# Loads moved to GpSimd's queue and stores to ACT's in a linear-attention and feed-forward kernel

## The chip, the cores and the metric

The kernel runs on one core of one Trainium2 chip. The metric is the device time of one execution in microseconds (us), as the median of several runs. Engines are PE (matmul), DVE (vector), ACT (scalar), POOL (GpSimd) and SP (sync, which here only issues transfers).

## The reference

```python
def phi(x):
    return np.where(x > 0, x, np.exp(x) - 1.0) + 1.0
q_p, k_p = phi(q), phi(k)                      # q, k, v: (8, 8, 576, 64) float32
kv  = np.einsum('bhsd,bhse->bhde', k_p, v)
z   = np.sum(k_p, axis=2)
num = np.einsum('bhsd,bhde->bhse', q_p, kv)
den = np.einsum('bhsd,bhd->bhs', q_p, z)[..., None] + 1e-06
x   = (num / den).transpose(0, 2, 1, 3).reshape(4608, 512)
h   = x @ w_in                                 # w_in: (512, 2048)
g   = 0.5 * h * (1.0 + np.tanh(np.sqrt(2 / np.pi) * (h + 0.044715 * h ** 3)))
out = g @ w_out                                # w_out: (2048, 512)
```

## The kernel before

Eight batches pass through a pipeline of first halves (x times w_in, then GELU) and second halves (g times w_out). A second half also prepares the attention of a batch two ahead. A main load is 512 of the 576 rows of one batch, 1 MB for each of q, k and v. The other 64 rows of two batches share one "remainder" tile. After GELU of half j the plan runs the functions that are registered for a slot (1 or 2 for first or second half, j, slot).

```python
def load_batch(b):                                   # all on SP
    if b % 2 == 0:
        ld["kr", b // 2] = load_rest(k, b // 2, "k_r", nc.sync)
    ld["k", b] = load_main(k, b, "k_x", nc.sync)
    ld["q", b] = load_main(q, b, "q_x", nc.sync)
    ...                                              # v and the remainders of v and q alike
def qtr():                                           # the transposed q of a batch, by DMA on SP
    phis("q")
    qts[b] = pt.tile([P, C, NP, P], BF16, name="qt")
    for c in range(C):
        nc.sync.dma_start_transpose(out=qts[b][:, c], in_=phi["q", b][:, c].rearrange(...))
def tx(c):                                           # the transposed x, by DMA on SP
    nc.sync.dma_start_transpose(out=xts[b][:, :, P * c : P * (c + 1)], in_=box["x", c]...)
def store(j, t, o_sb):                               # 512 KB of output, on GpSimd
    nc.gpsimd.dma_start(out=ov[:, t - 1 : t + 1, :], in_=o_sb)
...
at(1, 1, 15, lambda: load_batch(3))
plan_rest(0, (2, 1, 12), 2, 14)
for b in range(4, B):
    at(2, b - 3, 13 if b == 4 else 0, lambda b=b: load_batch(b))
```

Six load buffers of 1 MB are in rotation, so a load of batch b+2 can start as soon as the same load of batch b has been used. DMA transposes all go through SP's queue, in order.

## Time and profile before

| | before |
|---|---|
| time, median of three runs | 318.54 us (316.97 to 319.39) |
| PE busy | 290.1 us, 91% of a span of 318.6 us |
| DVE, ACT, POOL busy | 126.5, 153.9 and 27.8 us |
| mean granted PE clock | 0.970 |
| longest waits of PE | first GELU 7.5 us, transposed q of batch 4 6.4 us |

PE is the bound; what can be won is what it waits. The prediction shows the slices, the waits and the timelines. Two more lines: the table of DMA queues (packets, MB, share of 16 engines' time) and the table of DMA issues (count, median us from issue to landing).

```profile
q1 hardware_dynamic: 71968, 42.87, 49.1%
...
qt<-q_p SPq DMA_TRANSPOSE x24, 2.6
```

SP's queue, q1, carries nearly everything, and in the median a q transpose lands 2.6 us after its issue.

### The profile page before, as it was taken

Reading aid. Unit: us, or ns where it says so; the run is one execution under the profiler, and the core shown is the slowest. Engines: PE = TensorE matmul, PEld = TensorE weight load, DVE = VectorE, ACT = ScalarE, POOL = GpSimd, SP = SyncE. Lnnn points to the kernel's source line nnn. Section 1 sums busy time; section 2 is a strip of 40 time slices with the busy share of each in tenths; the row PEclk is TensorE's granted clock in tenths of the full one; section 3 lists DMA queues with packets and bytes.
Section 4 is the critical chain, followed back from the end, with each engine's and each line's share of the span. In section 5 each row is a group of like instructions: output and inputs, shape, how many; then the busy total and the mean of one; then the engine's idle time right before and its main releaser. Section 6 shows DMA issues by size and latency. Waiting matters only on the chain.

```text
span 318.6 us, 4203 instructions
## 1 busy us (share of the span) xinstructions
PE 290.1 (91%) x1624; PEld 147.7 (46%) x1652; DVE 126.5 (40%) x242; ACT 153.9 (48%) x214; POOL 27.8 (9%) x44
## 2 busy tenths in 40 slices
PE   8774588999999999929999999999999999999994
PEld 6552145444554544504445544544454444444443
DVE  3957255007787335912191439335523000000001
ACT  4636544678323576412844683557355036207500
POOL 6042261000000000000000000000100000000000
PEclk9998599999999999996999999999999999999998
DMA  7999999850484798993499259530623120011032
GB/s 246 343 377 260 386 328 321 270 177 0 144 171 128 191 340 118 300 260 84 109 357 262 49 153 359 134 60 6 137 74 66 43 95 0 2 66 67 0 68 68
DMA packets 75509, 52.72 MB, mean 165 GB/s; under 512 B 44128, under 2 KB 69984, under 8 KB 75488
## 3 DMA queue, kind: packets, MB, share of 16 engines
q1 hardware_dynamic: 71968, 42.87, 49.1%
q0 software_dynamic: 3360, 9.44, 9.5%
q8 instruction: 13, 0.21, 0.3%
q10 hardware_dynamic: 160, 0.13, 0.2%
q14 instruction: 8, 0.07, 0.1%
HBM read 36.70 MB, written 9.44 MB: 145 GB/s over the span
## 4 chain that ended last, share of the span: by engine, by line
PE 80%; DMA 11%; ACT 4%; DVE 2%; SPq 1%; issue 1%; DVEq 0%
PE o_ps L624 38%; PE h_ps L295 37%; DMA q_x<-in_q_dram 4%; DMA qt<-q_p 4%; PE n_ps L247 3%; DMA k_r<-in_k_dram 3%; PE kv_ps L212 2%; ACT g L587 1%; DMA out_dram<-o_sb 1%; SPq L67 1%; DVE vr L204 1%; ACT xt L548 1%; PE kv_ps L220 0%; ACT L140 0%; ACT kr_e L186 0%
## 5 line engine op out<-in xcount | busy, mean ns | idle before, releaser
L295 PE MATMUL h_ps<-xt,w_in_sb 128*128 128x512 bf16 (+1 forms) x513 | 124.1, 382 | 10.9 <-ACT g L587 8.2
L624 PE MATMUL o_ps<-w_out_sb,g 128*128 128x512 bf16 x548 | 122.5, 379 | 0.6
L587 ACT ACTIVATE g<-h_ps 128x512 bf16<-128x512 f32 x144 | 85.5, 598 | 62.7 <-PE h_ps L295 61.4
L295 PEld LDWEIGHTS <-w_in_sb 128*128 128x128 bf16 x592 | 56.7, 99 | 69.0 <-issue 16.5
L624 PEld LDWEIGHTS <-g 128*128 128x128 bf16 x560 | 54.5, 98 | 64.5
L638 ACT COPY o_sb<-o_ps 128x512 f32<-128x512 f32 x17 | 9.9, 585 | 66.4 <-issue 33.9
L636 DVE COPY o_sb<-o_ps 128x512 f32<-128x512 f32 x18 | 12.3, 685 | 63.0 <-PE o_ps L624 62.2
L565 POOL DMA_DIRECT2D out_dram<-o_sb x16 | 9.3, 584 | 229.9 <-DVE o_sb L636 120.2
L259 DVE TENSOR_TENSOR x<-n_ps,r 128x512 bf16<-128x512 f32 x36 | 24.9, 691 | 7.9 <-DMA xt<-x 6.5
L164 DVE TENSOR_SCALAR k_e<-k_e 128x2048 bf16<-128x2048 bf16 (+1 forms) x9 | 6.5, 717 | 41.0 <-ACT k_e L159 36.4
L257 DVE RECIPROCAL r<-n_ps 128x8 f32<-128x8 f32 x36 | 7.4, 206 | 36.4 <-PE n_ps L247 36.4
L168 DVE SCALAR_TENSOR_TENSOR q_p<-q_x,q_e 128x512 bf16<-128x512 f32 (+1 forms) x40 | 20.7, 579 | 0.3
L168 DVE SCALAR_TENSOR_TENSOR k_p<-k_x,k_e 128x512 bf16<-128x512 f32 (+1 forms) x36 | 20.3, 627 | 0.3
L247 PE MATMUL n_ps<-kvbd,qt 128*128 128x130 bf16 x128 | 13.1, 226 | 8.0 <-DMA qt<-q_p 6.4
L247 PEld LDWEIGHTS <-qt 128*128 128x128 bf16 x128 | 10.1, 101 | 15.1 <-DMA qt<-q_p 6.9
L236 DVE CAST kvbd<-kv_ps 64x260 bf16<-64x260 f32 (+1 forms) x17 | 6.7, 395 | 26.0 <-PE kv_ps L220 25.9
L295 PE MATMUL h_ps<-xt_rest,w_in_sb 128*128 128x512 bf16 x63 | 13.9, 379 | 0.1
L159 ACT ACTIVATE q_e<-q_x 128x2048 bf16<-128x2048 f32 x6 | 11.4, 1896 | 4.5 <-DVE q_p L168 4.5
L212 PE MATMUL kv_ps<-vp,k_p 128*128 128x130 bf16 x128 | 12.2, 220 | 1.5 <-DVE vp L196 1.5
L159 ACT ACTIVATE k_e<-k_x 128x2048 bf16<-128x2048 f32 x7 | 13.4, 1911 | 0.1
L321 PE MATMUL w_ps<-warm 128*128 128x252 bf16 x84 | 12.3, 310 | 1.1 <-DVE warm L122 1.1
L212 PEld LDWEIGHTS <-k_p 128*128 128x128 bf16 x128 | 9.5, 97 | 7.4 <-DVE vp L196 2.0
(54 smaller groups left out, 125.9 us busy)
## 6 DMA issues: line engine op xcount, KB each, us to landing
out_dram<-o_sb POOLq DMA_DIRECT2D x16, 512.0 KB, 3.3
k_x<-in_k_dram SPq DMA_DIRECT2D x7, 1024.0 KB, 6.1
v_x<-in_v_dram SPq DMA_DIRECT2D x7, 1024.0 KB, 10.0
q_x<-in_q_dram SPq DMA_DIRECT2D x6, 1024.0 KB, 9.5
w_st<-in_moe_w_out_dram SPq DMA_DIRECT2D x4, 1024.0 KB, 13.1
q_x<-in_q_dram SPq DMA_DIRECT2D x4, 512.0 KB, 10.5
w_st<-in_moe_w_in_dram SPq DMA_DIRECT2D x2, 1024.0 KB, 9.8
k_x<-in_k_dram SPq DMA_DIRECT2D x2, 512.0 KB, 4.2
```

Source lines behind the costliest of these rows:

```text
L159: nc.scalar.activation(e, ld[name, b], AF.Exp)
L168: nc.vector.scalar_tensor_tensor(xp[:, c, hs, :], xv[:, c, hs, :], 0.0, ev[:, c, hs, :], op0=ALU.max, op1=ALU.add,)
L212: nc.tensor.matmul(dst, lhsT=kp[:, c, P * i : P * (i + 1)], rhs=vps[b % 2][:, 2 * i : 2 * i + 2, c, :], start=(c == 0), stop=False,)
L247: nc.tensor.matmul(n_ps[rows, i // 2, 2 * E * (i % 2) : 2 * E * (i % 2) + 2 * E], lhsT=qt_c[:, i, rows], rhs=kvbd[:, i, :], skip_group_che ...
L259: nc.vector.tensor_tensor(x, n_v[:, :, :, 0:D], r[:, :, :, None].to_broadcast([P, 2, 4, D]), op=ALU.mult,)
L295: nc.tensor.matmul(h_ps[:, tok], lhsT=w_in_sb[:, c, P * m : P * (m + 1)], rhs=xt[:, c, tok], start=(c == 0), stop=(c == KM - 1), skip_grou ...
L321: nc.tensor.matmul(w_ps[:, 0:252], lhsT=warm[:, 0:P], rhs=warm)
L565: nc.gpsimd.dma_start(out=ov[:, t - 1 : t + 1, :], in_=o_sb)
L587: nc.scalar.activation(gs[j][:, m, :], h_ps, AF.Gelu_apprx_tanh)
L624: nc.tensor.matmul(o_ps, lhsT=g[:, m, P * t : P * (t + 1)], rhs=w_out_sb[:, m, :], start=(m == 0), stop=(m == MM - 1),)
L636: nc.vector.tensor_copy(dst, o_ps)
L638: nc.scalar.copy(dst, o_ps)
```

## The change

It is meant to shorten both long waits. The start gets the k remainder of batch 1 and its exponential earlier, and the later w_in loads behind a second cast. From batch 3 on, loads leave SP for GpSimd, so that SP has the transposes alone. GpSimd's stores go to ACT's queue. Two x transposes of the first group take another PSUM pool.

```diff
-    def load_batch(b):
+    def load_batch(b, eng):
         if b % 2 == 0:
-            ld["kr", b // 2] = load_rest(k, b // 2, "k_r", nc.sync)
-        ld["k", b] = load_main(k, b, "k_x", nc.sync)
+            ld["kr", b // 2] = load_rest(k, b // 2, "k_r", eng)
+        ld["k", b] = load_main(k, b, "k_x", eng)
 ... (q, v and their remainders alike)
     ld["k", 1] = load_main(k, 1, "k_x", nc.sync)
+    load_rest_half(k, ld["kr", 0], 0, 1, nc.sync)
 ...
     cast_w_in(0, nc.gpsimd.tensor_copy)
+    cast_w_in(1, nc.gpsimd.tensor_copy)
     load_w_in_cast(2)
-    cast_w_in(1, nc.gpsimd.tensor_copy)
     load_w_in_cast(3)
 ... (tx0: c < 2 from ps_ho as before, c >= 2 from ps_a)
-    load_rest_half(k, ld["kr", 0], 0, 1, nc.sync)
 ...
+    exp_rest_half("kr", kre, 1)
     phi["k", 1] = phi_of(ld["k", 1], ke, "k_p")
 ...
-    exp_rest_half("kr", kre, 1)
     gelu_table()
 ...
-    load_batch(2)
+    load_batch(2, nc.sync)
+    load_batch(3, nc.gpsimd)
 ...
-            nc.gpsimd.dma_start(out=ov[:, t - 1 : t + 1, :], in_=o_sb)
+            nc.scalar.dma_start(out=ov[:, t - 1 : t + 1, :], in_=o_sb)
 ...
-    at(1, 1, 15, lambda: load_batch(3))
 ...
-        at(2, b - 3, 13 if b == 4 else 0, lambda b=b: load_batch(b))
+        at(2, b - 3, 15, lambda b=b: load_batch(b, nc.gpsimd))
```

More of the change, by code (lines that the diff above doesn't have):

```diff
@@ L93 @@
     ld = {}
-    def load_batch(b):
+    def load_batch(b, eng):
         if b % 2 == 0:
-            ld["kr", b // 2] = load_rest(k, b // 2, "k_r", nc.sync)
-        ld["k", b] = load_main(k, b, "k_x", nc.sync)
-        ld["q", b] = load_main(q, b, "q_x", nc.sync)
+            ld["kr", b // 2] = load_rest(k, b // 2, "k_r", eng)
+        ld["k", b] = load_main(k, b, "k_x", eng)
+        ld["q", b] = load_main(q, b, "q_x", eng)
         if b % 2 == 0:
-            ld["vr", b // 2] = load_rest(v, b // 2, "v_r", nc.sync)
-        ld["v", b] = load_main(v, b, "v_x", nc.sync)
+            ld["vr", b // 2] = load_rest(v, b // 2, "v_r", eng)
+        ld["v", b] = load_main(v, b, "v_x", eng)
         if b % 2 == 0:
-            ld["qr", b // 2] = load_rest(q, b // 2, "q_r", nc.sync)
+            ld["qr", b // 2] = load_rest(q, b // 2, "q_r", eng)
     nc.scalar.preload_act_table_set("exp_and_others")
@@ L378, in tx0 @@
     def tx0(c):
-        t_ps = ps_ho.tile([P, NP, 2, P], BF16, name="t_ps", tag="ho")
-        t_x(x_c[c], t_ps[:, :, 0])
-        nc.scalar.copy(xt[:, :, P * c : P * (c + 1)], t_ps[:, :, 0])
+        if c < 2:
+            t_ps = ps_ho.tile([P, NP, 2, P], BF16, name="t_ps", tag="ho")[:, :, 0]
+        else:
+            t_ps = ps_a.tile([P, 4, NP, P], BF16, name="t_ps", tag="a")[:, 0]
+        t_x(x_c[c], t_ps)
+        nc.scalar.copy(xt[:, :, P * c : P * (c + 1)], t_ps)
     nab0(0)
```

## The prediction

> **What bounds the kernel now.** I read the page first, then the waits of the tensor engine, then the timelines of PE, of SP's queue, of ACT and of DVE around each long wait. The page's engine table gives PE 290.1 us of 318.6 us (91%), so only some 28 us can be won. The forty slices show where they lie:
>
> ```profile
> PE   8774588999999999929999999999999999999994
> ...
> PEclk9998599999999999996999999999999999999998
> DMA  7999999850484798993499259530623120011032
> ```
>
> PE is full except in the first seven slices (to about 56 us), in the eighteenth (135 to 143 us) and in the tail. The clock falls to half in just two places, behind the two long idles. The waits of PE name them (us in total, times, longest):
>
> ```profile
> PE h_ps L295 <- ACT g L587: 8.2, 2, 7.5
> PE n_ps L247 <- DMA qt<-q_p: 6.4, 1, 6.4
> PE kv_ps L212 <- DVE vp L196: 1.5, 1, 1.5
> ```
>
> The first wait, 27.24 to 34.73 us, is for the first GELUs. ACT reaches them late (start, duration, operation):
>
> ```profile
> 26.82 1.06 ACT L407 ACTIVATE q_e<-q_x 128x1024 bf16<-128x1024 f32 x1 [1.44 <-DMA q_x<-in_q_dram]
> 29.11 1.06 ACT L407 ACTIVATE q_e<-q_x 128x1024 bf16<-128x1024 f32 x1 [1.23 <-DMA q_x<-in_q_dram]
> 30.18 0.63 ACT L186 ACTIVATE kr_e<-k_r 64x512 bf16<-64x512 f32 x1
> 30.83 1.28 ACT L140 ACT_TABLE_LOAD   x1
> ```
>
> ACT waits for both halves of q of batch 1, then does the exponential of the k remainder, loads the table, and starts GELU at 32.12. The fifth GELU ends at 34.67 and releases PE.
>
> The second wait, 137.06 to 143.42 us, is for the first transposed q of batch 4. SP's queue shows why it is late:
>
> ```profile
> 107.67 0.55 SPq L67 DMA_DIRECT2D q_x<-in_q_dram  x1
> 108.27 3.53 SPq L76 DMA_DIRECT2D v_r<-in_v_dram  x2
> 111.91 1.67 SPq L67 DMA_DIRECT2D v_x<-in_v_dram  x1
> 113.67 3.93 SPq L76 DMA_DIRECT2D q_r<-in_q_dram  x2
> 117.71 6.08 SPq L488 DMA_TRANSPOSE xt<-x  x4
> ...
> 126.51 0.54 SPq L67 DMA_DIRECT2D k_x<-in_k_dram  x1
> 127.10 0.56 SPq L67 DMA_DIRECT2D q_x<-in_q_dram  x1
> 127.76 1.30 SPq L67 DMA_DIRECT2D v_x<-in_v_dram  x1
> 131.48 10.30 SPq L451 DMA_TRANSPOSE qt<-q_p  x4
> ```
>
> SP harms the transposes twice. Issuing batch 4's loads (105 to 117.6) keeps the xt transposes back, so their x buffers stay taken and DVE stands 6.5 us until 122.67; all of batch 4's elementwise work slides. Then three loads of 1 MB are issued just ahead of the qt transposes, the first of which lands 11.9 us after issue, where the median is 2.6.
>
> **What the skill says.** "DMA: Bandwidth & Descriptors", Queues, rings and completion order: an engine takes the descriptors of one ring in order and round-robins between rings at packet granularity. The trace agrees: a transpose behind 3 MB on its own ring waited 11.9 us, and from 22 to 34 us SP's ring and GpSimd's ring each filled about half the engines (61 and 57%, then 58 and 55%). The same page, Issuing engines are not separate DMA queues: another issuer adds no bandwidth. So the early loads get faster only if bytes ahead of them go away. "SBUF — State Buffer", SBUF: two separate sides: a VectorE operation in a two-port mode shuts GpSimd out of writing DMA descriptors. The trace shows the sharing with a GpSimd CAST: the DVE cast of vr at 43.85 took 2.01 us against a median of 0.43. For descriptor writing it shows nothing. "TensorE: Matmul & The Clock Gate", Part 1: about 3.4 us of idle halves the clock. The trace agrees: after 7.49 and 6.36 us of idle the granted clock was 0.50.
>
> **The change, part by part.**
>
> *a. The k remainder and its exponential move ahead of q of batch 1; the w_in loads on GpSimd wait for the second cast.* The w_in load that GpSimd issues at 18.98 flows from about 22 to 28 us and takes half the engines, just when w_in part 1 and q land on SP's ring (q's second half at about 29.1). After the change it is issued behind a cast that starts at about 23.3, so at about 25.2, and at the 3 us from issue to first bytes seen before it flows from 28. That returns about 3 us of DMA time to q. The moved remainder (128 KB in 256-byte pieces) takes back some 0.8 us. So q is complete at about 26.9 (29.1 less 2.2). ACT: the exponential of k ends at 25.4 as before, the remainder fills 25.4 to 25.9, the halves of q 25.9 to 28.0, the table to 29.3. GELU starts at 29.3 instead of 32.12: **2.8 us won**, 0.6 of it the reordering and 2.2 the arrival. PE still idles some 4.7 us and still runs its next matmuls at half clock, so I count no clock gain. The later w_in parts flow 28 to 34 and 34 to 40; m = 8 is needed at about 37.5 and m = 12 at about 42, so they should be just in time.
>
> *b. The banks.* Two x transposes take the two-bank pool in place of the four-bank pool. PE already ran m = 0 to 4 before the first GELU (8 half-width and 12 full matmuls from 23.62 to 27.24), and m = 5 waits for GELU 4 as before. I give it 0 us.
>
> *c. Loads of batches 3 to 7 leave SP.* The x transposes of batch 3 go out as DVE makes them, so DVE doesn't stand until 122.67. Batch 4's k work begins when ACT's exponential is done (117.51 + 1.91 = 119.4 in the old clock) instead of 123.27, its q_p appears some 3.9 us earlier, and the first qt transpose goes at about 127.5 and lands 2.6 us later, at 130. PE wants it at 137.06. The gap has 7 us of slack and goes: 6.36 us of idle, and the slow clock behind it. The chain goes from 143.42 to 147.44 for 4 n_ps and 8 h_ps matmuls, 4.02 us against 0.23 + 1.73 = 1.96 elsewhere, so 2.06 more. **8.4 us won.**
>
> *d. GpSimd's new work.* A load of 512 descriptors costs it 0.82 us and a store of 128 pieces 0.58. In a straight line, 1024 pieces cost about 1.2 us (estimate). 15 main loads and 12 half remainders are 15 x 1.2 + 12 x 0.8 = 28 us on an engine busy 27.8 of 318.6. Off the path.
>
> *e. 16 stores on ACT's queue.* At about 0.5 us each (SP's issue of a 1 MB load) plus up to 0.6 us waiting for its own copy, ACT loses about 1 us per store, in stretches where it is 45% busy. After a second half PE has three free banks, 2.6 us, before it needs the next GELU. About 0 us.
>
> Sum: 318.5 - 2.8 - 8.4 = 307.3. With nothing holding them, the loads start as soon as their buffers are free, that is while transposes of another batch run; I add back 1.2 us for leftover waits. **308.5 us.**
>
> **Rivals.** *1. The wait comes back as contention.* Round-robin now makes a transpose share every engine with a 3 MB load. For: the loads of batch b+2 start when batch b's q_p frees its buffer, which is when b's transposes run; x of batch 2 has only about 1 us of slack before 99.19 us. Against: load 4 is held by the q remainder's buffer until about 99, load 6's q and v wait for the same q_p, four free transposes take 5.2 us, and the slack at the old gap is 7 us. If it holds, 3 to 6 us of part c are lost: 311 to 314. *2. The start is held by something else.* If w_in's later parts land after 42 us, or GpSimd's casts collide with DVE's casts of v (the 1.5 us wait at 45.67), part a is eaten: about 311. *3. ACT becomes the bound through the stores.* If an issue on ACT blocks like SP's on a full queue (2 to 3.5 us), GELUs start late eight times: up to 8 x 2 us, and 318 or more. Against: one store has 128 rows a ring set must take, not 1024, and ACT has 52% free time. *4. Only the start, not the gap, was on the path.* The chain of waits passes through the qt transfer and PE is full afterwards, so I give this little.
>
> **Range and chances.** Both wins whole give 307; a warmer clock at the start could give 305. Rival 1 or 2 gives 311 to 314. The three runs of before lie 2.4 us apart. So 305.0 to 312.8. The 2% line is 312.2; both rivals together or rival 3 are needed to miss it: faster 0.87, within 2% 0.11, slower 0.02.
>
> **What would show it.** Right: GELU starts near 29.3; the wait of n_ps for qt near 130 us is gone and the clock there stays at 1; batch 4's first qt transpose goes right after DVE's q_p; PE's idle outside the start and tail is under 2 us. Wrong: waits of n_ps or h_ps for qt or xt in other stages (rival 1), a wait of h_ps for w_in near 38 to 44 us (rival 2), h_ps waiting for GELU at the start of each first half with ACT's queue at a store (rival 3). A GELU start that stays near 32 would make the prediction 3 us too low; a gap that only moves would make it 8 us too low.

## The result, and the profile after

The changed kernel takes 348.03 us (346.68 to 350.65, four runs) against 318.12 us for the kernel before in the same rounds. It is slower: the ratio is 1.0949, 95% interval 1.0861 to 1.1038. Ratios here are the mean time of one kernel's fast runs over that of the other's of the same rounds, so not quite the ratio of the medians quoted. The prediction was 308.5 us.

The forty slices of the changed kernel (busy tenths of PE, its granted clock, the share of the DMA engines):

```profile
PE   8884879996496999946999449999999999999995
...
PEclk9996999999697899976999879999999999999999
DMA  7999999549999943999229992163062211011023
```

Where the old kernel had one hole after the start, there are four (a slice is 8.6 us): in slices 10 and 11 (78 to 95 us), 13 (103 to 112), 18 and 19 (147 to 164) and 23 and 24 (190 to 207). The clock dips around each. The mean granted clock is 0.946. The waits of PE (us in total, times, longest):

```profile
PE n_ps L248 <- DMA qt<-q_p: 25.4, 7, 7.6
PE h_ps L296 <- ACT g L591: 5.4, 2, 4.7
PE h_ps L296 <- DMA xt<-x: 3.4, 1, 3.4
```

The span grew by 26.3 us. Waits for qt grew by 19.0 us, the wait for xt is 3.4 us and new, and the GELU wait is 2.8 us shorter. By difference 6.7 us remain, the net of slower matmuls after each hole and of smaller waits. The queues and the q transposes of this kernel:

```profile
q1 hardware_dynamic: 50032, 25.57, 36.7%
q0 software_dynamic: 5712, 18.35, 19.8%
q10 hardware_dynamic: 2464, 8.52, 7.1%
...
qt<-q_p SPq DMA_TRANSPOSE x24, 13.9
```

SP's ring carries less than before, yet its transposes land 13.9 us after issue instead of 2.6. SP's queue (start, duration, operation):

```profile
76.85 10.69 SPq L455 DMA_TRANSPOSE qt<-q_p  x4
...
103.38 12.05 SPq L455 DMA_TRANSPOSE qt<-q_p  x4
...
139.49 13.80 SPq L455 DMA_TRANSPOSE qt<-q_p  x4
...
180.26 14.85 SPq L455 DMA_TRANSPOSE qt<-q_p  x4
...
223.90 5.26 SPq L455 DMA_TRANSPOSE qt<-q_p  x4
```

Four transposes occupy SP for 10.7 to 14.9 us while there are loads to do, and for 5.26 us (1.31 each) in the last group, when there are none. GpSimd's timeline of the same stretch shows what they meet:

```profile
72.17 0.89 POOL L67 DMA_DIRECT2D k_x<-in_k_dram  x1 [21.12 <-ACT o_sb L642]
74.59 0.98 POOL L67 DMA_DIRECT2D q_x<-in_q_dram  x1 [1.52 <-DVE vp L197]
75.56 1.45 POOL L76 DMA_DIRECT2D v_r<-in_v_dram  x2
79.13 0.89 POOL L67 DMA_DIRECT2D v_x<-in_v_dram  x1 [2.12 <-issue]
80.06 1.37 POOL L76 DMA_DIRECT2D q_r<-in_q_dram  x2
```

These are batch 4's loads. In the program they stand at the end of the second half that begins at about 78 us. They go at 72 to 81 us, each when its buffer falls free, because with the stores gone nothing ahead of them in GpSimd's order waits for that stage. The old kernel issued them at 105 to 118 us on SP, behind batch 3's q transposes. They now flow with batch 2's q transposes, for which PE then waits 7.55 us, from 82.94 to 90.49.

The start did what was wanted. ACT's timeline:

```profile
22.38 1.91 ACT L160 ACTIVATE k_e<-k_x 128x2048 bf16<-128x2048 f32 x1
24.31 0.63 ACT L187 ACTIVATE kr_e<-k_r 64x512 bf16<-64x512 f32 x1
24.96 2.00 ACT L411 ACTIVATE q_e<-q_x 128x1024 bf16<-128x1024 f32 x2
...
28.28 2.06 ACT L591 ACTIVATE g<-h_ps 128x512 bf16<-128x512 f32 x4
```

The first GELU starts 5.90 us after the exponential of k, where before it was 8.65 us (23.47 to 32.12). The second half of the first batch starts at 64.35 us, some 5 us sooner than before. All of that and more is lost later.

### The profile page after: what moved, and what is told of

Its sections match the earlier page's. It is cut to its first block, busy times and chain, and to the rows that moved or that the text cites. A ratio compares the mean times of both kernels' runs of the same rounds, so it can differ in the third digit from the quotient of the medians.

```text
span 344.9 us, 4225 instructions
## 1 busy us (share of the span) xinstructions
PE 299.9 (87%) x1652; PEld 148.9 (43%) x1652; DVE 125.7 (36%) x242; ACT 153.6 (45%) x214; POOL 41.5 (12%) x55
## 4 chain that ended last, share of the span: by engine, by line
PE 49%; DMA 26%; DVE 12%; SPq 5%; ACT 3%; issue 3%; POOL 1%; DVEq 0%; ACTq 0%
PE h_ps L296 26%; PE o_ps L628 19%; DMA qt<-q_p 17%; DMA w_st<-in_moe_w_out_dram 4%; SPq L76 4%; DVE k_p L169 4%; DVE q_p L169 2%; ACT k_e L160 2%; PE n_ps L248 2%; DMA xt<-x 2%; DMA q_r<-in_q_dram 2%; DVE k_e L165 1%; PE kv_ps L213 1%; DVE vp L197 1%; DMA k_x<-in_k_dram 1%
## 5 line engine op out<-in xcount | busy, mean ns | idle before, releaser
L296 PE MATMUL h_ps<-xt,w_in_sb 128*128 128x512 bf16 (+1 forms) x528 | 130.9, 395 | 10.8 <-ACT g L591 5.4
L628 PE MATMUL o_ps<-w_out_sb,g 128*128 128x512 bf16 x560 | 124.4, 382 | 0.0
L296 PEld LDWEIGHTS <-w_in_sb 128*128 128x128 bf16 x592 | 57.9, 102 | 73.5 <-issue 19.3
L248 PE MATMUL n_ps<-kvbd,qt 128*128 128x130 bf16 x128 | 13.6, 232 | 27.0 <-DMA qt<-q_p 25.4
L165 DVE TENSOR_SCALAR k_e<-k_e 128x2048 bf16<-128x2048 bf16 (+1 forms) x9 | 5.7, 636 | 43.6 <-ACT k_e L160 38.9
L67 POOL DMA_DIRECT2D k_x<-in_k_dram x5 | 5.3, 1051 | 99.9 <-ACT o_sb L642 54.4
## 6 DMA issues: line engine op xcount, KB each, us to landing
k_x<-in_k_dram SPq DMA_DIRECT2D x2, 1024.0 KB, 10.3
```

The lines of the kernel that those rows point to most:

```text
L248: nc.tensor.matmul(n_ps[rows, i // 2, 2 * E * (i % 2) : 2 * E * (i % 2) + 2 * E], lhsT=qt_c[:, i, rows], rhs=kvbd[:, i, :], skip_group_che ...
L296: nc.tensor.matmul(h_ps[:, tok], lhsT=w_in_sb[:, c, P * m : P * (m + 1)], rhs=xt[:, c, tok], start=(c == 0), stop=(c == KM - 1), skip_grou ...
L628: nc.tensor.matmul(o_ps, lhsT=g[:, m, P * t : P * (t + 1)], rhs=w_out_sb[:, m, :], start=(m == 0), stop=(m == MM - 1),)
```

## The experiments

Three theories were set against each other. **P**: the loads from GpSimd meet the transposes, and since a DMA engine takes one packet from each ring in turn, a transpose of small packets waits for large ones. **A**: ACT's stores hold ACT or the transposes. **R**: GpSimd's work, and the loads it issues, are slow wherever they lie. Theory **C** came later: three rings at once are worse than two. In the texts T is P without its reason, "Rival S" is that the edits of the start do the harm, and "Theory G" is that the unheld loads with the remainders do it, whatever ring the stores take. "Ungated" means not held. Edits are against the changed kernel unless said otherwise, and some lines of them are left out.

### The start alone

```diff
 # loads back on SP at their old places, stores back on GpSimd
+    at(1, 1, 15, lambda: load_batch(3, nc.sync))
+        at(2, b - 3, 13 if b == 4 else 0, lambda b=b: load_batch(b, nc.sync))
+            nc.gpsimd.dma_start(out=ov[:, t - 1 : t + 1, :], in_=o_sb)
```

> Only the start of the change (k remainder and its exponential earlier, cast order, banks); loads of batches 3 to 7 on SP at their old places, stores on GpSimd. Theory T (transposes beside loads on another ring crawl; the start itself gained): 313.5 us, about 4.5 us under before, GELU start near 28.5 to 29.5, the wait of n_ps for qt of batch 4 still 6 to 7 us, no other wait for qt. Rival S (the start edits shift the whole schedule into the transposes' waits): over 320 us with new waits for qt.

It took 317.46 us against 317.95, ratio 0.9955 (0.9863 to 1.0047), where 313.5 was expected. The profile's span was 314.2 us, and its GELU wait fell to 5.4 us as in the changed kernel. So the mechanism is there, but the timed gain is not told from none. The old gap remained (a wait for qt of 5.7 us).

### Loads on SP, stores on ACT

```diff
-    load_batch(3, nc.gpsimd)
+    at(1, 1, 15, lambda: load_batch(3, nc.sync))
-        at(2, b - 3, 15, lambda b=b: load_batch(b, nc.gpsimd))
+        at(2, b - 3, 13 if b == 4 else 0, lambda b=b: load_batch(b, nc.sync))
```

> The change with the loads of batches 3 to 7 put back on SP at their old places; stores stay on ACT's queue. Theory T: as the start alone, 313.5 us, within 1 us of it. Rival A (stores on ACT's own ring, in 4 KB rows, slow the transposes or hold ACT up): 320 us or more, with waits for qt or of h_ps for GELU at the start of first halves.

It took 316.55 us, ratio 0.9948 (0.9898 to 0.9997), level with the start alone, and again above the 313.5 expected. The wait for qt was 5.5 us. Stores on ACT cost nothing by themselves: theory A falls in its simple form.

### Loads on GpSimd, stores back on GpSimd

```diff
-            nc.scalar.dma_start(out=ov[:, t - 1 : t + 1, :], in_=o_sb)
+            nc.gpsimd.dma_start(out=ov[:, t - 1 : t + 1, :], in_=o_sb)
```

> The change with only the stores back on GpSimd. GpSimd issues in order, so each batch of loads now stands behind the last store of the second half before it instead of going when buffers come free; the loads are still software DMA on their own ring. Theory T (it is the meeting in time of loads and transposes that costs): 305 to 309 us, the long waits of n_ps for qt at 90, 154, 161, 195 and 203 us gone, at most 3 us of waits for qt left. Rival R (software DMA loads are slow or harmful in themselves, wherever they lie): over 325 us.

It took 315.3 us, ratio 0.9820 (0.9741 to 0.9899, from the two of its four runs that were not slow; whether that is 2% faster than before stays unclear). This one line returns some 33 us. The 305 to 309 expected were missed, through a new wait. GpSimd's timeline and PE's longest new wait in this run:

```profile
98.41 0.53 POOL L569 DMA_DIRECT2D out_dram<-o_sb  x1 [7.98 <-ACT g L591]
98.95 1.41 POOL L76 DMA_DIRECT2D k_r<-in_k_dram  x2
100.35 0.90 POOL L67 DMA_DIRECT2D k_x<-in_k_dram  x1
101.24 0.89 POOL L67 DMA_DIRECT2D q_x<-in_q_dram  x1
...
PE n_ps L248 <- DMA qtr<-qr_p: 3.8, 1, 3.8
```

The same loads of batch 4 now go at 98.95 us and later, 26 us after those of the changed kernel. They stand behind a store, and a store waits for its output. There is no wait for qt left; a wait for the q remainder's transpose (qtr) of 3.8 us is new. GpSimd is busier here (50.7 us against 41.5), so theory R falls too. By itself this run does not separate "the loads are later" from "there are two rings and not three". The next one does.

### Three rings, but the loads held

```diff
+    def hold(cell):                       # a copy of one element of the newest o_sb into the load's buffer
+        if "o" in gate:
+            nc.gpsimd.tensor_copy(out=cell, in_=gate["o"])
     def load_main(src, b, name, eng, parts=1):
+        hold(t[:, 0, 0:1])                # and alike in load_rest; gate["o"] is set in second_half
```

> The change as it is, stores on ACT, but each load of batches 4 to 7 made to wait by data for the last output of the second half where the program places it (GpSimd copies one element of that output into the load's buffer first). Theory T: like the run with the stores on GpSimd, 305 to 309 us. Rival A (ACT's stores are part of the cost): 315 us or more while the run with the stores on GpSimd is near 307. Rival R: over 325 us.

It took 315.1 us, ratio 0.9925 (0.9860 to 0.9990); the 305 to 309 expected were missed here too. Stores stay on ACT and loads on GpSimd, all three rings are in use, and but for small copies on GpSimd only the time of the loads differs. The load of k of batch 4, which went at 72.17 us in the changed kernel, and the waits:

```profile
98.04 0.89 POOL L74 DMA_DIRECT2D k_x<-in_k_dram  x1 [0.30 <-POOL k_x L67]
...
PE n_ps L256 <- DMA qtr<-qr_p: 5.3, 1, 5.3
PE n_ps L256 <- DMA qt<-q_p: 1.5, 1, 1.5
```

The wait for qt falls from 25.4 us to 1.5. So the timing of the loads, which decides which transposes they meet, makes the difference of about 33 us.

### The rings by themselves

A bench: stages of six transposes on SP, alone or beside 3 MB of loads or stores that start with them. Its output is wrong, which doesn't matter for the time.

```diff
+    for i in range(3):
+        eng.dma_start(out=dst[i], in_=src_of_3_MB[i])      # eng: GpSimd, ACT or SP
+    for i in range(6):
+        nc.sync.dma_start_transpose(out=tr[i], in_=src)
```

> A bench that gives a wrong result on purpose: stages that start and end at a wait, each with 6 transposes of 128x512 bf16 from SP and 3 MB of loads (or stores) on some ring: GpSimd's or ACT's in 1 KB runs, both in 2 KB runs, ACT's in 256-byte runs, stores of 4 KB rows from ACT and from GpSimd, loads on SP itself ahead of the transposes, and transposes alone (first and last stage). Theory P (the engines take turns between rings packet by packet, so a transpose of 256-byte packets moves at the pace of the other ring's packets): alone about 1.3 us per transpose; beside GpSimd's loads, whose packets are near 4 KB, 5 to 9 us; beside ACT's 1 KB packets 2 to 3 us; beside ACT's 256-byte packets under 2 us; beside 4 KB stores of either ring 5 us or more. Rival Q (any load on another ring costs the same, by bandwidth): 2.5 to 3 us beside every load, GpSimd's and ACT's alike. Rival D (something of software DMA alone): 5 us or more beside GpSimd's ring, under 2 beside ACT's in every size.

Two answers for stretches of DMA (queue: packets, MB, share), beside GpSimd's loads at 46 to 50 us and beside the same loads on ACT at 62 to 64 us:

```profile
q0 software_dynamic: 312, 1.21, 89.2%
q1 hardware_dynamic: 312, 0.07, 10.0%
```

```profile
q10 hardware_dynamic: 540, 0.55, 82.3%
q1 hardware_dynamic: 453, 0.12, 26.6%
```

Beside GpSimd, both rings move exactly 312 packets in 4 us: turns of one packet each. GpSimd's packets are nearly all of 4 KB (1.21 MB over 312) and a transpose's of 256 B. At 78 to 90 packets per us, against 424 alone, the 544 packets of a transpose would take about 6.6 us instead of 1.31 if the loads lasted (an estimate; here they ended sooner, and the slowest transpose took 3.9 us from its first packet to its last, not the 5 to 9 expected). ACT carries the same loads in 1 KB packets, and the rings run at up to 283 packets per us each, which would be 1.9 us per transpose. While both rings have packets, the law of theory P holds, and the issuer's packet size sets the rate. The changed kernel shows it too, from 82 to 83 us:

```profile
q0 software_dynamic: 75, 0.25, 84.8%
q1 hardware_dynamic: 75, 0.02, 13.2%
```

The law is not all that the bench shows. From 41.1 to 45.0 us the transposes' ring moved 32 packets of 4 bytes beside 240 of GpSimd's: the second transpose began about 3 us later than one does alone, for a reason not found. The six took about as long in all beside either issuer (14 us, by the packet records). The 3 MB alone took 12.3 us from GpSimd and 11.5 from ACT.

### One load later, on SP

```diff
 # the start alone, and batch 5's loads behind batch 4's q transposes
-        at(2, b - 3, 13 if b == 4 else 0, lambda b=b: load_batch(b, nc.sync))
+        at(2, b - 3, {4: 13, 5: 6}.get(b, 0), lambda b=b: load_batch(b, nc.sync))
```

> The start of the change alone, everything on its old queue, but batch 5's loads are issued on SP after batch 4's transposes of q (slot 6 of that second half) instead of before them (slot 0). If the old gap came from the order on SP's ring: the wait of n_ps for qt (5.7 us in the run of the start alone) falls under 2 us and the time is 308 to 311 us. Rival (the gap comes from DVE being late, by the x buffers): the wait stays at 3 us or more and the time at 313 or more.

It took 313.33 us, ratio 0.9830 (0.9779 to 0.9881); the wait for qt fell from 5.7 us to 2.4, not under the 2 expected. Some 3 to 4 us of the old gap can be had with the loads left on SP, by order alone.

### A version that beats both

```diff
 # stores back on GpSimd as above, and one piece of attention a little later
-    plan_rest(0, (2, 1, 12), 2, 14)
+    plan_rest(0, (2, 1, 12), 3, 0)
```

> The change with the stores on GpSimd, and the attention of the first remainder moved from m = 14 of one first half to m = 0 of the next, so that its transposed q may land beside the loads. If that wait (3.8 us, and some 2 us of slow clock) was all that was left: 307 to 310 us by the profile, no wait for qt or qtr over 1 us. Rival (another wait of the same loads takes its place): 312 us or more and a new wait named in the profile.

It took **307.73 us** (306.83 to 310.77, five rounds), ratio 0.9682 (0.9629 to 0.9736). Its slices, and its two longest waits:

```profile
PE   8795678999999999999999999999999999999994
...
PE h_ps L296 <- ACT g L591: 5.4, 2, 4.7
PE kv_ps L213 <- DVE vp L197: 1.6, 1, 1.6
```

From the eighth slice to the last but one PE is at 9. No wait for a transfer of qt, qtr or xt is in the list. The old gap was to be had for about the sum that the prediction named (307.3 us), once the loads are held and this piece is moved, which the prediction did not contain.

### The banks

```diff
 # the start alone, without the bank change in tx0
```

> The start alone without the banks. If the banks are worth nothing: the wait of h_ps for the first GELUs stays at 4.5 to 5 us, and from the end of the last x copy to the first GELU the same 5.9 us pass as in the start alone. If they matter: one of the two is longer by 0.5 us or more.

In one look, the GELU wait was 5.4 us in total and 4.7 at longest, the same as with the banks, and from the exponential of k to the first GELU it was 5.91 us. The banks are worth nothing that shows.

### Small runs on GpSimd's ring

```diff
+    # bench 2: loads in 256-byte runs from GpSimd beside the transposes, then with ACT's stores as a third ring
```

> The second bench, wrong result on purpose, same form (6 transposes on SP per stage): transposes alone; GpSimd loads in the remainders' form (256-byte runs into 64 partitions) alone; the same beside transposes; ACT loads of that form beside transposes; GpSimd loads of 256-byte runs into 128 partitions beside transposes; GpSimd 1 KB-run loads and ACT stores both beside transposes. The first bench showed one transpose packet per packet of the other ring. If GpSimd packs 16 pieces of 256 bytes into one packet, such a packet is slow and the transposes fall to 60 packets per us or less (9 us each) beside the remainders; if it sends them one by one, they run at 200 or more. Beside two busy rings of 4 KB packets: 40 to 60 packets per us.

GpSimd packs 256-byte runs into 4 KB packets as well. Beside them the transposes moved 55 to 382 packets per us (by whole us from 39 to 51), about 2 us each; the 60 expected as the ceiling was missed. GpSimd's issue left gaps. The stage with ACT's stores is invalid: they ran early.

### The remainders off GpSimd

```diff
-            ld["kr", b // 2] = load_rest(k, b // 2, "k_r", eng)
+            ld["kr", b // 2] = load_rest(k, b // 2, "k_r", nc.sync)    # v and q alike
```

> The change with only the remainders' loads (256-byte runs) put back on SP, at the places of the change; the main loads stay ungated on GpSimd. If the main loads' 4 KB packets are the main cost: still 335 to 347 us, with waits for qt of 15 us or more. If the remainders' pieces on GpSimd's ring are the main cost: 320 to 330 us, waits for qt under 8 us.

It took 326.02 us, ratio 1.0221 (1.0140 to 1.0302), as expected for a cost that lies mostly with the remainders. The q transposes at 75 to 100 us, median from issue to landing, in the changed kernel and then here with PE's wait:

```profile
qt<-q_p SPq DMA_TRANSPOSE x4, 14.9
```

```profile
qt<-q_p SPq DMA_TRANSPOSE x4, 8.3
...
PE n_ps L248 <- DMA qt<-q_p: 7.8, 4, 2.6
```

The loads of 1 MB are about as early as in the changed kernel (75.08 us for k of batch 4), and some three quarters of the loss against the kernel before are gone. So meeting the large packets of these loads is not all of it.

### The queues alone

```diff
 # the kernel before, with the new queues and places of loads and stores, but without the new start
```

> The kernel before with only the queue change (loads of batches 3 to 7 on GpSimd, stores on ACT), without the edits of the start. If the two parts add up: 3 to 5 us over the change, 350 to 353 us, first GELU near 32, waits for qt near 25 us. If the start's earlier times caused the meeting of loads and transposes: under 340 us.

It took 353.59 us with a wait for qt of 30.5 us. Three of the four runs were slow, the profiled one too, so this size is not used. The one fast run took 347.22 us, level with the changed kernel and under the 350 to 353 expected. The sign is plain: the queues do the harm without the new start.

### The order of casts alone

```diff
 # against the kernel before
     cast_w_in(0, nc.gpsimd.tensor_copy)
+    cast_w_in(1, nc.gpsimd.tensor_copy)
     load_w_in_cast(2)
-    cast_w_in(1, nc.gpsimd.tensor_copy)
```

> The kernel before with only the order of GpSimd's second cast and first w_in load exchanged. From the exponential of k of batch 1 to the first GELU: 8.65 us before, 5.90 in the change. If the order of the casts frees the DMA engines for q (2.2 us of my 2.8): 6.4 to 6.6 us here, as ACT still does the k remainder after q. If the moved remainder was what counted: 8 us or more.

ACT's timeline:

```profile
23.13 1.91 ACT L159 ACTIVATE k_e<-k_x 128x2048 bf16<-128x2048 f32 x1
...
29.74 2.56 ACT L587 ACTIVATE g<-h_ps 128x512 bf16<-128x512 f32 x5
```

From the exponential of k to the first GELU it is 6.61 us: 2.0 of the 2.75 us come of the casts alone, and the other 0.7, by difference, of the moved remainder and its exponential.

### Three rings in a bench

```diff
+    # bench 3: GpSimd's loads, SP's transposes and ACT's stores at once
```

> Third bench, wrong result on purpose, 8 transposes a stage: alone; GpSimd 1 KB-run loads of 3 MB with four ACT stores of 512 KB, no transposes; the same beside transposes (three rings); the same with the stores on GpSimd's ring (two rings); GpSimd loads alone beside transposes; alone. Theory C (three rings at once, one of them writing to HBM, is what makes the traffic collapse): in the three-ring stage the transposes fall under 50 packets per us, with transpose packets of 0.2 us and longer, and the stage takes far longer than the stage with the stores on GpSimd's ring, which keeps 80 per us. Rival P (one packet each per turn, nothing more): about 45 to 55 packets per us with three rings, 80 with two, all packets of their usual length (0.018 and 0.16 us), and total traffic stays near 350 GB/s.

For about 2 us all three ran at full turns, with some 60, 47 to 56 and 26 to 52 packets per us. With two rings it was 80 to 109 each. No collapse: theory C was not seen. The overlap was short, as each store waited for rows that an earlier one wrote.

### Stores on SP, loads free on GpSimd

```diff
-            nc.scalar.dma_start(out=ov[:, t - 1 : t + 1, :], in_=o_sb)
+            nc.sync.dma_start(out=ov[:, t - 1 : t + 1, :], in_=o_sb)
```

> The change with only the stores moved from ACT's queue to SP's, so behind the transposes on their ring; the loads stay ungated on GpSimd. Theory C (the third ring makes the collapse): 318 to 330 us and waits for qt of at most 12 us. Theory G (the ungated loads with the remainders on GpSimd make it, the stores' ring is nothing): 342 to 350 us, waits for qt over 20 us.

It took 323.51 us, ratio 1.0165 (1.0134 to 1.0196), inside the 318 to 330 expected by theory C. The same landing figure for 75 to 100 us, the waits, and a stretch of DVE:

```profile
qt<-q_p SPq DMA_TRANSPOSE x4, 9.4
...
PE n_ps L248 <- DVE r L258: 5.8, 1, 5.8
PE n_ps L248 <- DMA qt<-q_p: 3.1, 3, 1.3
...
95.37 0.69 DVE L640 COPY o_sb<-o_ps 128x512 f32<-128x512 f32 x1 [11.51 <-DMA out_dram<-o_sb]
```

Again the loads are as early and unheld. Taking ACT's ring away removes most of the wait for qt, as taking the remainders away did. The new wait of 5.8 us comes of DVE, which stood 11.51 us until an earlier store on SP had landed and its output buffer was free; the reading of n_ps is next in DVE's order.

### Both taken away

```diff
 # stores on SP and the remainders' loads on SP
```

> The change with both the remainders' loads and the stores on SP; only the main loads stay on GpSimd, ungated. If what is then left is the turn by turn of 4 KB load packets alone (6.6 us a transpose where they meet): 314 to 323 us, waits for qt of 2 to 8 us. If it stays over 330, some part of the main loads' cost is not explained by packets taking turns.

It took 327.54 us, three of four runs and the profiled one slow, with waits for qt of 2.9 us and for xt of 7.5. DVE stood again for a store on SP, 9.2 us. The one fast run took 319.25 us, inside the 314 to 323 expected if only turns are left, but one run is too little. It settles nothing on theory C.

### The mixture in a bench

```diff
+    # bench 4: eight transposes on SP; GpSimd's 3 MB, remainders and ACT's strided stores (rows of their own), added one by one
```

> A bench, wrong on purpose: eight transposes on SP's queue in each of six stages, alone (1), beside 3 MB of loads on GpSimd with three ACT stores of 512 KB whose rows lie in one piece (2), the same with the ACT stores strided as in the change (3), the same with the remainders on GpSimd as well (4), the loads and remainders without stores (5), alone (6). Each ACT store writes rows that no earlier one wrote, so none waits. If the collapse in the change comes of the mixture of ACT's strided stores and the remainders, stage 4 (perhaps 3) shows transpose packets under 60 per us and single packets over 0.2 us, and a transpose takes over 9 us there, where stages 2 and 5 keep 80 to 90 packets per us and 6 to 7 us. If it needs something that only the whole kernel has, all three-ring stages stay at one packet each in turn, 45 to 60 per us while the stores last and 80 to 90 after, and no stage takes over 9 us for a transpose.

The second stage, with three rings, from 23 to 29 us:

```profile
q0 software_dynamic: 297, 1.15, 56.7%
q10 hardware_dynamic: 243, 0.93, 42.7%
q1 hardware_dynamic: 248, 0.06, 5.1%
```

Some 41 to 50 packets per us on each ring, 357 GB/s in all: a nearly equal share of three. The transpose that met it took 10.3 us from its first packet to its last (22.52 to 32.82, by the packet records). In this the second theory's "no stage takes over 9 us" was wrong. Strided rows and remainders made no difference that resembles the changed kernel: with everything at once, from 71 to 75 us, the rings moved 216, 209 and 186 packets. The changed kernel from 150 to 158 us reads otherwise:

```profile
q0 software_dynamic: 155, 0.57, 41.9%
q1 hardware_dynamic: 389, 0.09, 25.5%
q10 hardware_dynamic: 68, 0.26, 8.7%
```

In 8 us, fewer packets than the bench moved in 6, at 118 GB/s in all. Some packets are long: by the records of 149 to 160 us, a 256-byte packet took 0.105 us in the mean, with 1.05 at most; in the bench it was 0.020. The median is 0.018 in both, so the mean is made by a few. In the whole changed kernel 964 of 34816 such packets took over 0.2 us. In the kernel before it was 61 of 40960, and with the loads held, or the remainders or the stores on SP, 177 to 364.

So there are two parts to the loss: the equal turns, which the benches and the kernel show, and slow single packets, which every run has and the changed kernel has most of. The second part is **not settled**. The runs say that it needs early loads (the gated kernel lost most of it), and that either the remainders on GpSimd or the stores on ACT suffice to be taken away for most of it to go. Why is open: the kept trace does not say which of the 16 engines moved a packet.

## Why the prediction was wrong

**Part a, the start: right in mechanism and size.** 2.8 us were predicted from the exponential of k to GELU, and 2.75 measured, split 2.0 and 0.7 against 2.2 and 0.6. GELU started 1 us earlier than named because k's exponential itself began 1.1 us sooner in this run (22.38 us against 23.47). That moment varies: in the profiles of kernels with the very same start it lies between 22.38 us (the changed kernel) and 26.11 (one load later). So 2.8 us at the start are smaller than what the start varies by, and the start alone gave only 0.5 us in the medians, within ±0.9%.

**Part b, the banks: right**, 0 us.

**Part c, the gap: right on what could be won, wrong on what the change would do.** With the loads held the gap closes, but the kernel takes 315.3 us (or 315.1, gated), as a wait for qtr appears that the prediction had not. Only with a piece of attention moved as well does it take 307.73 us against the sum's 307.3, so that this agreement is in part luck. In the change as written the loads aren't held, and the slack of 7 us that the step counted on for the first transpose was spent: the transposes that took 2.6 us to land took 13.9.

**Part d, GpSimd's work: right.** It was put at 28 us of new issue time less the stores that leave (16 x 0.58, so some 19 us net). Measured: 13.7 more, with 0.88 to 0.98 us for most loads of 1 MB instead of the estimated 1.2. Off the path.

**Part e, stores on ACT: right** taken alone, as the run with loads on SP shows. ACT's issues took 0.34 to 0.39 us each. The step missed the other side of the move: kept on GpSimd, a store that waits for its output holds the loads behind it, as the run with the stores back on GpSimd shows. Moving the stores took this brake off.

**The step that failed** is the end of the sum: "With nothing holding them, the loads start as soon as their buffers are free, that is while transposes of another batch run; I add back 1.2 us for leftover waits." The event was named and its price was wrong: in place of 1.2 us there are waits of 25.4 us for qt and 3.4 for xt, and the slower matmuls behind them. **Rival 1** was the right one in kind, with 3 to 6 us where the loss beyond the sum was about 41 (348.03 less 307.3). Its counter-arguments failed one by one. "Load 4 is held by the q remainder's buffer until about 99" was false: k, q and v of batch 4 went at 72 to 81 us, as their own buffers fell free. "Load 6's q and v wait for the same q_p" was no help: they went at 137.90 and 141.78 us, beside the transposes from 139.49. "Four free transposes take 5.2 us" was true only without loads: 10.7 to 14.9 with them.

The root is a quantity that was not worked out. The prediction cited the rule of turns at packet granularity from the Trainium skill, and checked it by shares of engine time of two plain loads (the 61 and 57% given are those of 22.5 to 28 us; from 22 us on they are 65 and 52%). It never asked how large a packet is on each ring. Fair turns share packets, not bytes or time: 4 KB against 256 B leaves a transpose a sixteenth of the bytes. From the law alone a transpose beside loads takes 6.6 us instead of 1.31, and 3 MB of loads are 768 such packets, enough to delay one and a half transposes, 7 to 8 us per batch (an estimate). That would have been far above 1.2. The median landing in fact came 11.3 us later (13.9 against 2.6); the third ring and the slow packets are the candidates for the rest, and their shares are not shown.

**Rivals 2, 3 and 4.** No wait of note for w_in appeared, no GELU was late by a store, and the gap was on the path. The chances (0.02 for slower) came of taking rival 1's size for its bound.

## What to carry to other kernels

Before a load moves to another issuing engine, work out which transfers it will then meet and in what packets: here a transfer in 256-byte packets moved 78 packets per us beside a full ring of 4 KB packets, and 424 alone. And ask what held the load before: on an in-order queue the work ahead of a transfer is its brake, and moving that work away sends the transfer early. Here a store kept in front of the loads was worth some 33 us. With it, and with the piece of attention moved, the kernel came to 307.73 us; whether that piece moved alone, with the loads left on SP, would do as well was not tried.

## What the Trainium skill lacked or had wrong

- "DMA: Bandwidth & Descriptors", Queues, rings and completion order, has the turns at packet granularity right (312 packets against 312 in 4 us). It gives 9 to 17 descriptors as typical for a packet, and under SWDGE vs HWDGE vs iDMA 4096 B as the preferred limit on GpSimd's path; the 4 KB seen here agree. It gives no size on trn2 for the other issuers: the same load goes in packets of 1 KB on ACT's or SP's ring, and a transpose in 256 B. That difference sets the rate of a transpose, 78 packets per us beside GpSimd's loads against up to 283 beside ACT's.
- The same page, Rules for kernel authors, says that spreading over SP, ACT and GpSimd "only saves sequencer issue time", and, in a row on wrong results, that a transpose next to ordinary DMAs needs nothing. For results that holds: every variant of the kernel gave the right output. For time it doesn't: the issuer of the stores, one line, moved the median landing of q transposes from 2.4 to 13.9 us and the kernel from 315.3 to 348.0.
- No page accounts for the number of slow packets in the changed kernel: 964 of 34816 packets of 256 B took over 0.2 us, against 61 of 40960 in the kernel before. The cause is open.
- "SBUF — State Buffer", Who interferes with whom, warns that a VectorE operation can starve GpSimd of descriptor writing. That is not wrong, and there are small signs of it: the load issued at 177.35 us took GpSimd 1.67 us beside a cast of DVE that began at 177.32, where most loads took 0.88 to 0.98. In the kernel before, stores took 0.70 and 0.71 us beside such casts (128.58, 163.35) and 0.53 in most other places, so that the prediction's "For descriptor writing it shows nothing" missed a small sign. It decided nothing here.
